# Long-convolution weights on TensorE: half-zero weights replaced by full ones

## The chip, the core and the metric

The kernel runs on one core of one Trainium2 chip. The metric is device time in microseconds (us); lower is better. The engines are named as in the profile: PE (TensorE matmul) and PEld (its weight loads), DVE (VectorE), ACT (ScalarE), POOL (GpSimd) and SP (SyncE, which here only issues DMAs).

## What is computed

Two independent halves are computed and concatenated along the last axis, each of shape 1 x 2048 x 512, in bf16.

```python
# A: attention, 32 heads of 16
qkv = (x @ wqkv).reshape(B, S, 3, 32, 16)
p = softmax(einsum("bhqd,bhkd->bhqk", q, k) * 16 ** -0.5)
a = einsum("bhqk,bhkd->bhqd", p, v).reshape(B, S, 512) @ wo
# B: gated long convolution, 512 channels
k_shift = sum_t k_pad[:, t:t+S] * shift_k[:, 3 - t]        # 4 taps
kv = k_shift * v
y = causal_conv(kv, ssm_k) + kv * ssm_D                     # 2048 taps per channel
b = q * y
```

The reference does the causal convolution by FFT; the kernel does it directly on PE.

## The kernel before

**Attention.** There are 2,048 blocks of scores, each 128 keys by 512 queries of one head (line 679). A loop over steps T (line 1429) emits the program; it is a planner written in Python that keeps a model time for each engine and decides at build time which instruction comes next on which engine. Each step takes up to three blocks into one of two sets of three PSUM banks (`emit_qk`, L796 is the scores matmul); ACT turns the whole set into exponentials with one instruction (L821), 128 x 1536 for three blocks or 128 x 1024 for two, into places of the ring PT. Two steps later the products with V follow (L970), four heads side by side in column groups, all accumulated in bank PVB; each finished group of 64 blocks is transposed on DVE (L1041).

**Blocks on DVE.** DVE computes the exponential of some blocks itself. `dve_block` chooses one, `exp_on_dve` emits it: L884 reads the scores out of PSUM, then on pairs of blocks follow four kinds of steps, `mant` (L892, into FR), `power` (L896), `line` (L899), `square` (L902) and `cube` (L905). The result has three parts, so each such block needs three product matmuls (ring PTD, R_PTD = 3 pairs of three tiles). A DVE block comes either beside a full set of three ACT blocks, in bank BGB, or in place of the third ACT block, in its bank (`own`, lines 726 to 730; this is tried when the DVE work in store is under LOW). BGB is refused while a convolution burst or a unit holds it (`busy`), and while a burst wants to begin (`conv_wants`).

**The convolution.** The zero-padded, reversed filters lie in HBM as kz_scratch. `feed_wr` (L1157) loads the rows of the ring WR: partition i of the lower 64 holds the filter of one channel shifted by i, the upper 64 partitions the filter of the channel 64 rows further on. `conv_lags` (L1187) multiplies, for a group `qd` of 8 channels, KV (weights) with WR (moving): KV has the time blocks of one channel on the lower and of the other channel on the upper half, in alternate columns, with zeros in the other half of each column. 64 groups x 32 lags x 4 column groups make 8,192 matmuls. Two groups form a burst in BGB; its end is a copy with reversed order to YB on DVE (L1207). After every fourth group four transposes (L1219, the "turn") and one product with Q (L1226) follow.

**Inputs of the convolution.** Units `("kv", c, i)` compute the 4-tap shift as matmuls with diagonal weights (L512) and multiply with V on DVE (L561, two instructions per unit); `spread_kv` then spreads the result over the partitions with four DMAs per unit group.

**Order.** Other background work comes as units with due steps (`jobs`, from PLAN steps). `emit_bg` gives the convolution up to LAGS = 10 lags per step if the room before the next ACT end allows it. `release` issues filter rows by the modelled DMA rate (WR_KB, line 122) and so that they do not collide with PE's fetches of its own code. A burst may begin only WAIT = 3.0 us (line 106) after the modelled landing of its rows (line 1337). Where nothing else fits, `warm_up` (L1382) puts filler matmuls on PE. The last N_TAIL = 9 steps have two blocks each.

Of the kernel before, what the change touches and what calls it, by code (L numbers as in the profile page):

```python
# [27 lines left out]
NLAG = S // 64  # L28
# [4 lines left out]
R_W = 12  # L33
R_PT = 16
# [8 lines left out]
LEAD = 2  # L43
YIELD = -4
FIRST = 6
BURST = 2
OVER_C = 0.0
HURRY = 2
LOW = 4.5
# [20 lines left out]
R_PTD = 3  # L70
# [12 lines left out]
PLAN = 588  # L83
# [4 lines left out]
GAP = 5  # L88
# [7 lines left out]
DMA_KB = 394  # L96
X_KB = 200
# [157 lines left out]
def bass_concat_heads__mha_block__ssm_conv_h3__prompt_kernel(  # L255
# [24 lines left out]
    def sb(name, shape, dt=BF16):  # L280
# [9 lines left out]
    WR = sb("WR", [128, R_W, S])  # L290
    WRF = WR[:, :, :].rearrange("p r w -> p (r w)")
    KV = sb("KV", [128, C // 8, 2, 2 * NB, 4])
    QNF = sb("QN", [128, NB * 256 + 2 * LEFT])
    QN = QNF[:, 0:NB * 256].rearrange("p (t d) -> p t d", t=NB)
# [13 lines left out]
    PTD = sb("PTD", [128, R_PTD, 3, 2, QB])  # L308
    FR = sb("FR", [128, 2 * QB])
# [7 lines left out]
           for x in (WR[:, R_W - 2, :], WR[:, R_W - 1, :], OUTA[:, :, :].rearrange("p r d -> p (r d)"), VS2[:, :])]  # L317
# [9 lines left out]
    KVF = KV[:, :, :, :, :].rearrange("p o r u g -> p (o r u g)")  # L327
    STG = [KVF[:, 32 * S // 16 * ((c + 1) % 4):32 * S // 16 * ((c + 1) % 4 + 1)].rearrange(
        "p (h o u k g) -> p h o u k g", h=2, o=16, u=NB, k=2) for c in range(4)]
    XN = FR[:, :].rearrange("p (j f) -> p j f", j=2)  # L330
# [66 lines left out]
    d_wr = [DmaSem(sem(f"d_wr{i}")) for i in range(3)]  # L397
# [25 lines left out]
    for c in range(4):  # L423
        src = bass.AP(tensor=v2.tensor, offset=v2[128 * (NB - 1), 128 * c].offset, ap=[[D, 128], [-128 * D, NB], [1, 128]])
        h_vn.append(dma(sp, d_kv[3 + c], VST[c], src, kb=512))
# [18 lines left out]
    h_kv0 = [None, None]  # L444
    h_kv0[0] = pool.op(lambda e: e.memset(KV[:, :, :, :, :].rearrange("p o r u g -> p (o r u g)").bitcast(U32), 0), us=(8.8, 8.9))
# [25 lines left out]
    def ready(u):  # L471
        if u[0] == "q":
            return (u[1] < R_Q or 2 * (u[1] - R_Q) + 1 in qk_done) and (u[1] < 2 or 2 * u[1] - 1 in h_q and at(h_q[2 * u[1] - 1]) <= pe.t + 0.5)
        if u[0] == "k":
            return u[1] < 2 or LAST[u[1] - 2] in qk_done
        if u[0] == "v":
            return u[1] < 2 or LAST[u[1] - 2] in pv_done
        if u[0] == "op":
            return (PAIRS.index((3, u[1])) if u[1] < NQB - 1 else (15, u[2] + 1)) in h_otn and h_wop[0] is not None
        return KT_OF[u[1]][0] in h_kt and (u[1] < 3 or h_kv0[1] is not None and at(h_kv0[1]) <= pe.t)  # L480

    def pe_unit(u, bank, parts=(0, 1, 2, 3)):
# [19 lines left out]
        elif kind == "kv":  # L502
# [5 lines left out]
            def mm(e, b):  # L508
                ins = None
                for m in range(4):  # L510
                    c0 = LEFT + 128 * (4 * i + 3 - b) - m
                    ins = e.matmul(PS[:, bank, 128 * b:128 * b + 128], lhsT=KTR[kt_i][:, kt_c, c0:c0 + 128], rhs=DG[:, c, m, :],  # L512
                                   start=(m == 0), stop=(m == 3))
# [20 lines left out]
    def evac_unit(u, bank, h):  # L534
# [18 lines left out]
        elif kind == "kv":  # L553
            _, c, i = u
            u0 = NB - 4 - 4 * i
            val = VST[c][:, u0:u0 + 4, :].rearrange("p b (h o g) -> p b h o g", h=2, g=4)
            src = PS[:, bank, :].rearrange("p (b h o g) -> p b h o g", b=4, h=2, g=4)
            for ch in range(2):
                dst = STG[c][:, ch, :, u0:u0 + 4, ch, :].rearrange("p o u g -> p u o g")
                hh = (dve.op if ch else urgent)(  # L560
                    lambda e, dst=dst, ch=ch: e.tensor_tensor(dst, src[:, :, ch], val[:, :, ch], ALU.mult),  # L561
                    [h, h_vn[c], h_kv0[c // 3]], us=(0.335, 0.46))
# [3 lines left out]
            if sum(kv_n[0:2]) == 8 and c < 2:  # L566
                load_qn(0, [h])
                open_wr(2, hh, True)
# [13 lines left out]
    def spread_kv(c, hh):  # L582
        for half in range(2):
            for ch in range(2):
# [23 lines left out]
    def kz_store(us):  # L608
# [4 lines left out]
        open_wr(R_W - 2, h_kzw[0])  # L613
# [111 lines left out]
    def emit_qk(T):  # L725
# [12 lines left out]
        bl = next_blocks(n + (extra in next_blocks(n)))  # L738
        if extra in bl:
            bl.remove(extra)  # L740
# [30 lines left out]
    def next_blocks(n):  # L771
        bl = []
        for b in [b for b in queue[:LOOK] if blk_group(b) == blk_group(queue[0])] + queue[:n]:
            if len(bl) < n and b not in bl and (blk(b)[2] not in [blk(x)[2] for x in bl] or len(bl) + 1 > 4):
                bl.append(b)
        for b in queue[:n]:
# [58 lines left out]
    def conv_due():  # L835
        return N_OPEN + state["qd"] * (PLAN - N_OPEN) / (C // 8)

    def conv_wants(T):
        qd = state["qd"]
        return (state["started"] and T >= conv_due() - YIELD and qd < C // 8 and wr_next[0] >= qd + BURST and h_kvc[qd // 16] is not None  # L840
                and at(h_wr[qd + BURST - 1], h_kvc[qd // 16]) + WAIT < pe.t + 1.0 and not (state["turn"] and qd % 4 == 4 - BURST))

# [3 lines left out]
    def dve_block(T, n_act, aside=True):  # L846
        if T < T_DVE or aside and busy() or len(queue) < LAST_BLKS + 3 * TAIL_GAP + 4:
            return None
        if aside and conv_wants(T):
# [9 lines left out]
        bl = next_blocks(n_act + 1)  # L859
        x = sub(bl[-1])  # L860
        left = len([b for b in queue if sub(b) == x])
        if left - 3 >= 2.6 * GAP:
            return bl[-1]
# [6 lines left out]
        rows = [blk(b)[2] for b in bl[:-1]]  # L870
        ahead = [b for b in ahead[:4] if b not in bl]
        return next((b for b in ahead if blk(b)[2] not in rows), ahead[0] if ahead else None)
# [5 lines left out]
    def exp_on_dve(b, bank, h):  # L878
# [4 lines left out]
        lin, low, top = [PTD[:, j % R_PTD, i, :, :].rearrange("p a n -> p (a n)") for i in range(3)]  # L883
# [7 lines left out]
        def mant(us):  # L891
            st["d"] = st["m"] = dve.op(lambda e: e.tensor_scalar(FR[:, w].bitcast(U16), lin[:, w].bitcast(U16), 0x7F, 0x3F80, ALU.bitwise_and, ALU.bitwise_or),  # L892
                                       [st["h"][-1], h_last.get(j - 1)], us=us)

        def power(us):
            dve.op(lambda e: e.tensor_scalar(low[:, w].bitcast(U16), lin[:, w].bitcast(U16), 0xFF80, None, ALU.bitwise_and), [st["h"][-1]], us=us)  # L896

        def line(us):
            st["d"] = dve.op(lambda e: e.tensor_scalar(top[:, w].bitcast(FP16), FR[:, w], T1, T0, ALU.mult, ALU.add), [st["m"]], us=us)  # L899

        def square(us):
            st["d"] = h_last[j] = dve.op(lambda e: e.tensor_tensor(top[:, w].bitcast(FP16), FR[:, w], top[:, w].bitcast(FP16), ALU.mult), [st["d"]], us=us)  # L902
# [6 lines left out]
        begin = lambda: (n == 2 or st["alone"]) and (j == 0 or j - 1 in h_last)  # L909
        if half == 0:  # L910
            flow.append([])
            st["f"] = flow[-1]
        st["f"][:] = [("p", dep, mant, FOUR[n], begin), ("p", lambda: [st["h"][-1]], power, FOUR[n], lambda: True), ("p", lambda: [st["m"]], line, FOUR[n], lambda: True),
                      ("p", dep, square, TWO[n], lambda: True), ("p", dep, cube, TWO[n], lambda: True)]
# [26 lines left out]
    def emit_pv(bl, T):  # L941
# [5 lines left out]
        for b in bl:  # L947
            n, _, s = blk(b)
            pv_n[(n, s)] = pv_n.get((n, s), 0) + 1
            terms = [PTD[:, on_dve[b][0] % R_PTD, i, on_dve[b][1], :] for i in range(3)] if b in on_dve else [PT[:, pt_of[b], :]]  # L950
# [567 lines left out]
```

## Time and profile before

| | |
|---|---|
| median of 3 runs | 815.03 us (811.89 to 816.54) |
| the profiled execution | 807.64 us |
| its span in the profile | 805.7 us |
| busy: PE / DVE / ACT / POOL | 745.7 / 715.1 / 784.9 / 90.4 us |
| granted PE clock, mean | 0.999 |

A line of the groups reads: line, engine, operation, output <- input, shapes, number; then busy time in us and mean length of one in ns; then the idle time of the engine just before these instructions and who ended it. Instructions overlap on an engine's pipeline, so number times mean can exceed busy time. A line of the waits reads: who waited <- for whom: us in total, times, longest. A line of the timeline reads: start, length, engine, line, operation, number merged.

### The profile page before, as it was taken

What the parts mean: (1) busy time and instruction counts of PE and PEld (TensorE: products, weight loads), DVE (VectorE), ACT (ScalarE), POOL (GpSimd) and SP (SyncE); (2) the same over time, 40 slices, a digit from 0 to 9 for tenths busy, and PEclk for the clock granted to TensorE, in tenths of its full rate; (3) what the DMA queues carried; (4) which work ended last, traced back from release to release, by engine and by line L of the source; (5) the groups of instructions that cost most, each with busy time, mean ns of one, the idle gap of its engine ahead of it and who ended that gap; (6) DMA issues with size and microseconds to landing.
All of it is one profiled execution on the core that took longest, in us unless ns stands there. A gap on an engine that the chain in (4) does not pass through costs nothing.

```text
span 805.7 us, 31982 instructions
## 1 busy us (share of the span) xinstructions
PE 745.7 (93%) x14505; PEld 337.1 (42%) x14505; DVE 715.1 (89%) x1427; ACT 784.9 (97%) x680; POOL 90.4 (11%) x160
## 2 busy tenths in 40 slices
PE   8889998999998989999999989989989899999987
PEld 3333444435444433444433434434443434434444
DVE  5989999999798989898898989889999899889986
ACT  7999999999999999999999999999999999999997
POOL 6200402020100101020010030101003020000000
PEclk9999999999999999999999999999999999999999
DMA  9995277846877671446845657985684663876310
GB/s 244 204 306 175 63 184 227 287 108 215 265 261 240 215 243 59 156 115 235 267 142 206 213 168 254 308 281 193 227 299 138 212 224 129 283 260 216 110 55 28
DMA packets 88101, 161.44 MB, mean 200 GB/s; under 512 B 49216, under 2 KB 53184, under 8 KB 87584
## 3 DMA queue, kind: packets, MB, share of 16 engines
q1 hardware_dynamic: 80976, 150.43, 58.2%
q0 software_dynamic: 5792, 8.66, 3.7%
q8 instruction: 114, 1.87, 0.9%
q10 hardware_dynamic: 1200, 0.33, 0.2%
q14 instruction: 19, 0.16, 0.1%
HBM read 142.87 MB, written 6.42 MB: 185 GB/s over the span
## 4 chain that ended last, share of the span: by engine, by line
ACT 79%; PE 14%; DVE 5%; issue 1%; DMA 1%
ACT PT L821 79%; PE PS L970 5%; PE PS L796 4%; PE PS L1187 1%; DVE PTD L884 1%; DMA QN<-in_B_k_dram 1%; PE PS L512 1%; PE PS L1115 1%; PE PS L630 0%; PE PS L491 0%; DVE PTD L902 0%; DVE DT L1041 0%; DVE PTD L905 0%; DVE FR L892 0%; DVE PTD L896 0%
## 5 line engine op out<-in xcount | busy, mean ns | idle before, releaser
L821 ACT ACTIVATE PT<-PS 128x1024 bf16<-128x1024 f32 (+1 forms) x674 | 781.9, 1362 | 11.5 <-PE PS L796 10.8
L796 PE MATMUL PS<-QT,KTo 32*128 32x512 bf16 (+2 forms) x2248 | 265.6, 364 | 39.8 <-ACT PT L821 17.5
L884 DVE TENSOR_SCALAR PTD<-PS 128x512 uint16<-128x512 f32 x326 | 219.2, 682 | 49.2 <-PE PS L796 47.8
L1187 PE MATMUL PS<-WR,KV 128*26 128x128 bf16 (+9 forms) x8192 | 191.2, 219 | 0.7 <-issue 0.6
L970 PE MATMUL PS<-PT,VA 128*32 128x512 bf16 (+2 forms) x1889 | 184.6, 369 | 5.0 <-DVE DT L1041 2.1
L1187 PEld LDWEIGHTS PS<-WR,KV 128*32 128x32 bf16 (+8 forms) x8192 | 140.6, 94 | 52.9 <-issue 29.8
L796 PEld LDWEIGHTS PS<-QT,KTo 32*128 32x128 bf16 x2248 | 69.6, 91 | 205.0 <-ACT PT L821 150.4
L970 PE MATMUL PS<-PTD,VA 128*32 128x512 bf16 (+1 forms) x1077 | 121.0, 360 | 3.9 <-issue 3.9
L902 DVE TENSOR_TENSOR PTD<-FR,PTD 128x1024 f16<-128x1024 bf16 (+1 forms) x164 | 112.3, 685 | 4.0
L905 DVE TENSOR_TENSOR PTD<-PTD 128x1024 bf16<-128x1024 f16 (+1 forms) x164 | 111.5, 680 | 1.9
L352 POOL DMA_DIRECT2D QT<-QS x120 | 60.4, 511 | 443.7 <-DVE QS L539 443.7
L970 PEld LDWEIGHTS PS<-PT,VA 128*32 128x32 bf16 x1889 | 47.4, 93 | 100.8 <-issue 85.5
L892 DVE TENSOR_SCALAR FR<-PTD 128x1024 uint16<-128x1024 uint16 (+1 forms) x164 | 69.0, 421 | 3.5
L896 DVE TENSOR_SCALAR PTD<-PTD 128x1024 uint16<-128x1024 uint16 (+1 forms) x164 | 68.9, 420 | 0.0
L1382 PE MATMUL PS<-IDN,ZW 128*32 128x512 bf16 (+3 forms) x297 | 67.4, 310 | 1.3 <-issue 1.0
L899 DVE TENSOR_SCALAR PTD<-FR 128x1024 f16<-128x1024 bf16 (+1 forms) x164 | 68.1, 415 | 0.0
L970 PEld LDWEIGHTS PS<-PTD,VA 128*32 128x32 bf16 x1077 | 44.8, 96 | 33.2 <-issue 4.4
L1382 PEld LDWEIGHTS PS<-IDN,ZW 128*32 128x32 bf16 x297 | 23.4, 96 | 23.3 <-issue 12.2
L1041 DVE STREAM_TRANSPOSE DT<-PS 128x512 f32<-128x512 f32 x31 | 22.1, 713 | 5.6 <-PE PS L970 5.3
L352 POOL DMA_DIRECT2D out_dram<-OUTA x15 | 8.6, 575 | 97.2 <-DVE OUTA L1123 93.1
L1115 PE MATMUL PS<-WKV,OTN 128*128 128x512 bf16 (+1 forms) x68 | 19.0, 371 | 0.3 <-DVE OTN L1090 0.3
L523 PE MATMUL PS<-WKV,xT 128*128 128x128 bf16 x256 | 18.3, 220 | 0.4 <-DVE KTo L548 0.3
(75 smaller groups left out, 259.3 us busy)
## 6 DMA issues: line engine op xcount, KB each, us to landing
WR<-kz_scratch SPq DMA_DIRECT2D x256, 512.0 KB, 5.8
KV<-KV SPq DMA_DIRECT2D x16, 256.0 KB, 5.4
kz_scratch<-WR SPq DMA_DIRECT2D x1, 2176.0 KB, 8.8
QN<-in_B_q_dram POOLq DMA_DIRECT2D x2, 1024.0 KB, 7.6
out_dram<-QN POOLq DMA_DIRECT2D x2, 1024.0 KB, 8.3
QT<-QS POOLq DMA_DIRECT2D x120, 16.0 KB, 3.3
out_dram<-OUTA POOLq DMA_DIRECT2D x15, 128.0 KB, 2.0
QN<-in_B_ssm_k_dram SPq DMA_DIRECT2D x1, 1024.0 KB, 8.3
```

Of the source, the lines that this page charges most:

```text
L352: f(outp, inp).then_inc(dsem.sem, 16)
L796: ins = e.matmul(PS[:, bank, i * w:i * w + w], lhsT=KTo[32 * s:32 * s + 32, OF[n_] % 2, kt * 128:(kt + 1) * 128], rhs=QT[32 * s:32 * s + 3 ...
L821: h_exp[T] = act.op(lambda e: e.activation(PT[:, p0:p0 + n, :].rearrange("p b f -> p (b f)"), PS[:, banks[0]:banks[0] + n, :].rearrange("p ...
L884: st["h"].append(urgent(lambda e: e.tensor_scalar(lin[:, QB * half:QB * half + QB].bitcast(U16), PS[:, bank, :], FIX_ADD, FIX_HI, ALU.add, ...
L892: st["d"] = st["m"] = dve.op(lambda e: e.tensor_scalar(FR[:, w].bitcast(U16), lin[:, w].bitcast(U16), 0x7F, 0x3F80, ALU.bitwise_and, ALU.b ...
L896: dve.op(lambda e: e.tensor_scalar(low[:, w].bitcast(U16), lin[:, w].bitcast(U16), 0xFF80, None, ALU.bitwise_and), [st["h"][-1]], us=us)
L899: st["d"] = dve.op(lambda e: e.tensor_scalar(top[:, w].bitcast(FP16), FR[:, w], T1, T0, ALU.mult, ALU.add), [st["m"]], us=us)
L902: st["d"] = h_last[j] = dve.op(lambda e: e.tensor_tensor(top[:, w].bitcast(FP16), FR[:, w], top[:, w].bitcast(FP16), ALU.mult), [st["d"]], ...
L905: st["d"] = dve.op(lambda e: e.tensor_tensor(top[:, w], top[:, w].bitcast(FP16), lin[:, w], ALU.mult), [st["d"]], us=us)
L970: ins = e.matmul(dst, lhsT=w, rhs=rhs, start=first, stop=last, tile_position=(0, 32 * s))
L1187: ins = e.matmul(PS[32 * g:32 * g + 2 * ((30 - d) // 2 + 1), BGB, c0:c0 + w], lhsT=kv, rhs=WR[:, (4 * qd + g) % R_W, S - 64 * d - 128:S - ...
L1382: pe.op(lambda e, s=s, k=k, rhs=rhs, bank=bank, rows=rows, c0=c0, first=first: e.matmul(PS[32 * s:32 * s + rows, bank, c0:c0 + 128 * k], l ...
```

## The change

Each channel's 2,048 time steps are now 32 blocks of 64. The lower 64 partitions of WR hold lags of one channel, the upper 64 the lags 1024 further on of the same channel; KV holds on its upper half the same time blocks 1024 earlier, so no weight is zero by construction, apart from the blocks before the start of time. A group `qd` is 4 channels, there are 128 groups of 8 steps, and each matmul covers two lags of 64, whose results are added when YB is turned: the turn is now two matmuls with permuted identity columns per 128 columns instead of one transpose, into fp32. Four groups form a burst.

A filter row of WR is half as long (1,024 columns); a DMA writes 64 partitions of two rows. The ring has 24 rows of half the length, so the same bytes. The kv units write KV directly with one DVE instruction, and one DMA per unit group makes the upper half. Q and the convolution's output move in two DMAs each, 128 channels wide.

Beside that, the blocks on DVE get other rings (R_PTD = 5 for the first tile, R_RST = 3 for the two others; FR is gone and `mant` writes into the second tile, `power` comes after `square`), PT has 14 places instead of 16, blocks are chosen so that the blocks of a step lie in different head rows (`next_blocks`, `pick_row`), `conv_wants` refuses a DVE block only if the last attempt found room for lags or the convolution is over 30 steps behind, and several planner constants have other values.

```diff
-NLAG = S // 64
+NLAG = S // 256
+NQD = C // 4
-R_W = 12
-R_PT = 16
+R_W = 24
+R_PT = 14
+PRESS = 30
-FIRST = 6
-BURST = 2
+FIRST = 4
+BURST = 4
-LOW = 4.5
+LOW = 3.5
-R_PTD = 3
+R_PTD = 5
+R_RST = 3
-PLAN = 588
+PLAN = 600
-GAP = 5
+GAP = 7
...
-    PTD = sb("PTD", [128, R_PTD, 3, 2, QB])
-    FR = sb("FR", [128, 2 * QB])
+    PTD = sb("PTD", [128, R_PTD, 2, QB])
+    RST = sb("RST", [128, R_RST, 2, 2, QB])
...
 kv unit
-                    c0 = LEFT + 128 * (4 * i + 3 - b) - m
-                    ins = e.matmul(PS[:, bank, 128 * b:128 * b + 128], lhsT=KTR[kt_i][:, kt_c, c0:c0 + 128], rhs=DG[:, c, m, :],
-                                   start=(m == 0), stop=(m == 3))
+                    for x in range(2):
+                        c0 = LEFT + 64 * (4 * i + 3 - b) + S // 2 * x - m
+                        ins = e.matmul(PS[64 * x:64 * x + 64, bank, 128 * b:128 * b + 128], lhsT=KTR[kt_i][:, kt_c, c0:c0 + 64],
+                                       rhs=DG[:, c, m, :], start=(m == 0), stop=(m == 3), tile_position=(0, 64 * x))
...
 spread_kv
-        for half in range(2):
-            for ch in range(2):
-                src = STG[c][64 * half:64 * half + 64, ch].rearrange("p o u k g -> p o (u k g)")
-                dst = KV[ch:128:2, 16 * c:16 * c + 16, 1 - half, :, :].rearrange("p o u g -> p o (u g)")
-                h_kvc[c] = dma(sp, d_kvc[c], dst, src, [hh, h_kvc[c - 1] if c else None] if half + ch == 0 else [], kb=256, rate=210)
+        src = KV[0:64, 32 * c:32 * c + 32, 0:NB, :].rearrange("p q w g -> p q (w g)")
+        dst = KV[64:128, 32 * c:32 * c + 32, NB:2 * NB, :].rearrange("p q w g -> p q (w g)")
+        h_kvc[c] = dma(sp, d_kvc[c], dst, src, [hh, h_kv0, h_kvc[c - 1] if c else None], kb=256, rate=KV_KB)
...
 dve_block
-        if aside and conv_wants(T):
+        if aside and conv_wants(T) and (state["go"] or conv_due() < T - PRESS):
...
 feed_wr
-            qd, g = n // 4, n % 4
-            row = 128 * (qd // 16) + 4 * (qd % 16) + g
-            src = bass.AP(tensor=kz_ap.tensor, offset=kz_ap[row, 0].offset, ap=[[1, 64], [64 * LKZ, 2], [1, S]])
-            h_wr[qd] = dma(sp, d_wr[qd % 3], WR[:, n % R_W, :], src, [h_kzw[0], dep, h], kb=512, rate=WR_KB, late=2.95)
+            qd, r, x = n // 4, n % 4 // 2, n % 2
+            src = bass.AP(tensor=kz_ap.tensor, offset=kz_ap[channel(qd) + 2 * r, S // 2 * x].offset, ap=[[1, 64], [LKZ, 2], [1, S // 2]])
+            n0 = (4 * qd + 2 * r) % R_W
+            h_wr[qd] = dma(sp, d_wr[qd % (R_W // 4)], WR[64 * x:64 * x + 64, n0:n0 + 2, :], src, [h_kzw[0], dep, h], kb=256, rate=WR_KB, late=2.95)
...
 conv_lags
-                d = DIST[n]
-                w = 64 if d < 0 else 128
                 for g in range(4):
-                    kv = KV[:, qd, (1 + d) % 2, (1 + d) // 2 * 2:2 * NB, g]
-                    ins = e.matmul(PS[32 * g:32 * g + 2 * ((30 - d) // 2 + 1), BGB, c0:c0 + w],
-                                   lhsT=kv, rhs=WR[:, (4 * qd + g) % R_W, S - 64 * d - 128:S - 64 * d - 128 + w],
+                    dst = PS[32 * g:32 * g + 32 - 2 * n, BGB, :]
+                    c0 = 256 * (1 - pair) + 64 * (1 - half)
+                    dst = bass.AP(tensor=dst.tensor, offset=PS[32 * g:32 * g + 1, BGB, c0:c0 + 1].offset, ap=[dst.ap[0], [128, 2], [1, 64]])
+                    w0 = S // 2 - 128 * n - 128
+                    ins = e.matmul(dst, lhsT=KV[:, channel(qd) // 4, 2 * n:2 * NB, g], rhs=WR[:, (4 * qd + g) % R_W, w0:w0 + 128],
                                    start=(n == 0), stop=(n == NLAG - 1), tile_position=(0, 32 * g))
...
 conv_turn
-                ins = e.transpose(pbf[:, 128 * k:128 * k + 128], YB[:, b % 2, 128 * k:128 * k + 128], IDN[:, :])
+                for part in range(2):
+                    y = YB[:, k // 2, 256 * (k % 2) + 128 * part:256 * (k % 2) + 128 * part + 128]
+                    ins = e.matmul(PS[:, bank, 128 * k + 4 * part:128 * k + 128], lhsT=y, rhs=(own, next_)[part], start=part == 0, stop=part == 1)
```

More of the change, by code (lines that the diff above doesn't have):

```diff
@@ L479, in ready @@
             return (PAIRS.index((3, u[1])) if u[1] < NQB - 1 else (15, u[2] + 1)) in h_otn and h_wop[0] is not None
[L480 removed]
+        return KT_OF[u[1]][0] in h_kt
     def pe_unit(u, bank, parts=(0, 1, 2, 3)):
@@ L869, in dve_block @@
             return None
-        rows = [blk(b)[2] for b in bl[:-1]]
-        ahead = [b for b in ahead[:4] if b not in bl]
-        return next((b for b in ahead if blk(b)[2] not in rows), ahead[0] if ahead else None)
+        return pick_row(ahead, 4)
     h_last = {}
@@ L908, in exp_on_dve @@
         dep = lambda: [st["d"]]
-        begin = lambda: (n == 2 or st["alone"]) and (j == 0 or j - 1 in h_last)
+        begin = lambda: (n == 2 or st["alone"]) and (j < R_RST or all((j - R_RST, i) in h_ptd for i in range(len(pairs[j - R_RST]["h"]))))
         if half == 0:
@@ L949, in emit_pv @@
             pv_n[(n, s)] = pv_n.get((n, s), 0) + 1
-            terms = [PTD[:, on_dve[b][0] % R_PTD, i, on_dve[b][1], :] for i in range(3)] if b in on_dve else [PT[:, pt_of[b], :]]
+            terms = [PT[:, pt_of[b], :]] if b not in on_dve else [PTD[:, on_dve[b][0] % R_PTD, on_dve[b][1], :]] + [
+                RST[:, on_dve[b][0] % R_RST, i, on_dve[b][1], :] for i in range(2)]
             hl = 2 * s + n % 2
@@ L991, in conv_done @@
     def conv_done():
-        return state["qd"] == C // 8 and not state["turn"] and not part[0]
+        return state["qd"] == NQD and not state["turn"] and not part[0]
     def pv_step(T):
@@ L1213, in conv_turn @@
     def conv_turn(b, bank):
-        pbf = PS[:, bank, :].bitcast(BF16)
+        own, next_ = [bass.AP(tensor=IDN[:, :].tensor, offset=IDN[0:1, 31:32].offset, ap=[IDN[:, :].ap[0], [-1, n], [32, 4]]) for n in (32, 31)]
         def fn(e):
```

163 lines of the change are left out of this document (86 added, 77 removed).

## The prediction

> **What bounds the kernel now.** I read the engine totals first, then the chain that ended last, then the groups with their forms kept apart, then the waits.
>
> ```profile
> PE 745.7 (93%) x14505; PEld 337.1 (42%) x14505; DVE 715.1 (89%) x1427; ACT 784.9 (97%) x680; POOL 90.4 (11%) x160
> ...
> ACT 79%; PE 14%; DVE 5%; issue 1%; DMA 1%
> ...
> L821 ACT ACTIVATE PT<-PS 128x1024 bf16<-128x1024 f32 (+1 forms) x674 | 781.9, 1362 | 11.5 <-PE PS L796 10.8
> ```
>
> ScalarE (ACT) is occupied for 784.9 of 805.7 us, and the chain runs through it for 79% of the span. Its exponential (L821) loses 11.5 us to idling in all, nearly all of it waiting for scores (L796). So the time can fall in two ways only: ACT idles less, or ACT gets less to do. The forms show what its work is made of:
>
> ```profile
> L821 ACT ACTIVATE PT<-PS 128x1536 bf16<-128x1536 f32 x374 | 524.9, 1558 | 2.8 <-PE PS L796 2.5
> L821 ACT ACTIVATE PT<-PS 128x1024 bf16<-128x1024 f32 x300 | 301.1, 1117 | 8.7 <-PE PS L796 8.3
> ...
> L884 DVE TENSOR_SCALAR PTD<-PS 128x512 uint16<-128x512 f32 x326 | 219.2, 682 | 49.2 <-PE PS L796 47.8
> ...
> L902 DVE TENSOR_TENSOR PTD<-FR,PTD 128x1024 f16<-128x1024 bf16 x162 | 111.4, 688 | 4.0
> L905 DVE TENSOR_TENSOR PTD<-PTD 128x1024 bf16<-128x1024 f16 x162 | 110.6, 683 | 1.9
> ...
> L892 DVE TENSOR_SCALAR FR<-PTD 128x1024 uint16<-128x1024 uint16 x162 | 68.4, 422 | 3.4
> L896 DVE TENSOR_SCALAR PTD<-PTD 128x1024 uint16<-128x1024 uint16 x162 | 68.3, 422 | 0.0
> L899 DVE TENSOR_SCALAR PTD<-FR 128x1024 f16<-128x1024 bf16 x162 | 67.6, 417 | 0.0
> ```
>
> There are 2,048 score blocks. ACT takes 374 x 3 + 300 x 2 = 1,722, VectorE (DVE) the other 326. A third block makes an ACT instruction 1558 - 1117 = 441 ns longer. 1,722 x 0.441 = 759.4 us; the remaining 22.5 us of the 781.9 are spread over 674 instructions, 33 ns each. So **a block moved to DVE is worth 0.441 us, an instruction saved 0.033 us**. A block costs DVE 682 + (688 + 683 + 422 + 422 + 417)/2 = 1,998 ns, say 2.0 us. DVE is 89% busy, and over half of its 90.6 idle us, 47.8, is spent in front of L884 with no block of scores at hand. What DVE lacks is blocks in time; that is where the change has to act.
>
> Now what the convolution takes from TensorE (PE):
>
> ```profile
> L1187 PE MATMUL PS<-WR,KV 128*26 128x128 bf16 (+9 forms) x8192 | 191.2, 219 | 0.7 <-issue 0.6
> ```
> ```profile
> 210.92 0.29 PE L1187 MATMUL PS<-WR,KV 128*26 128x128 bf16 x8
> ...
> 213.75 0.74 PE L1187 MATMUL PS<-WR,KV 128*16 128x128 bf16 x40
> 214.74 0.71 PE L1187 MATMUL PS<-WR,KV 128*6 128x128 bf16 x40
> 216.27 0.73 PE L1187 MATMUL PS<-WR,KV 128*28 128x128 bf16 x40
> ```
>
> Four column groups run side by side: 32 more matmuls lengthen a run by 0.45 us, 14 ns each, whether the weights have 6, 16 or 28 columns. 8,192 of them are 115 us of PE's pace, the largest part that isn't attention.
>
> **The change, part by part.**
>
> *Convolution on PE.* 64 x 32 lags x 4 become 128 x 8 x 4 = 4,096 matmuls. The weights that remain are the wide ones (32 to 18 columns), which the rows above show to cost no more. Gain: 57 us.
>
> ```profile
> L523 PE MATMUL PS<-WKV,xT 128*128 128x128 bf16 x256 | 18.3, 220 | 0.4 <-DVE KTo L548 0.3
> ...
> L512 PE MATMUL PS<-OTN,QN 128*128 128x128 bf16 x128 | 9.4, 220 | 1.6 <-DMA QN<-in_B_k_dram 1.0 <-DVE KV L561 0.3 <-DVE PTD L884 0.3
> L512 PE MATMUL PS<-OTN 128*128 128x128 bf16 x128 | 9.2, 220 | 0.7 <-DVE KV L561 0.7
> ```
>
> *Turn and kv units on PE.* The turn (L1219) gets 128 matmuls for 64; at the 18.3/256 = 71 ns of L523 that is +4.6 us. The kv units (L512) get 512 half-wide ones for 256; in two column groups they should run in pairs as the convolution's fours do, so +0; one after the other they would cost another 18.6 us. I take 0. PE sheds about 57 - 5 = 52 us. None of that is saved time by itself: PE isn't the bound, and the warm-up filler (L1382) will occupy part of it.
>
> *DVE.* The copy from PSUM (L1207) stays at 32 instructions but doubles to 512 columns:
>
> ```profile
> L1207 DVE CAST YB<-PS 128x256 bf16<-128x256 f32 x32 | 13.3, 416 | 5.8 <-PE PS L1187 3.0 <-PE PS L970 2.3 <-PE PS L1382 0.4
> ...
> L575 DVE CAST VA<-PS 128x512 bf16<-128x512 f32 x16 | 10.9, 681 | 1.5 <-PE PS L523 1.5
> ...
> L561 DVE TENSOR_TENSOR KV<-PS,WR 128x256 bf16<-128x256 f32 x16 | 6.0, 413 | 2.0 <-PE PS L512 2.0
> ```
>
> 32 x (681 - 416) = +8.5 us. The kv products (L561) go from 32 of 413 ns to 16 of about 681: -2.3 us. The other DVE steps of a pair keep their number and shape. Net +6.2 us of DVE work.
>
> *Rings of DVE blocks.* The first result of a pair gets five places instead of three, the other two tiles get their own ring of three, and the shared FR tile with its order between pairs is gone. Two more pairs are four L884, 2.7 us of work that can be taken while the ring behind is full.
>
> ```profile
> DVE PTD L884 <- PE PS L796: 47.8, 67, 3.3
> ```
>
> The longest of these 67 waits is 3.3 us, so most fit into that lead; but the four fifths of the arithmetic that follow still wait for a ring of three. I take 30 of the 47.8 us as gained (ends: 0 and 47.8).
>
> *The bank BGB.* DVE blocks beside a full ACT instruction need this bank, and a convolution burst holds it:
>
> ```profile
> 208.87 0.24 PE L1187 MATMUL PS<-WR,KV 128*32 128x128 bf16 x1
> ...
> 226.68 0.25 PE L1187 MATMUL PS<-WR,KV 128*32 128x128 bf16 x1
> ```
> ```profile
> 222.80 0.41 DVE L1207 CAST YB<-PS 128x256 bf16<-128x256 f32 x1
> ...
> 238.16 0.42 DVE L1207 CAST YB<-PS 128x256 bf16<-128x256 f32 x1
> ```
>
> 13.9 and 11.5 us are held in bursts that come 15 to 18 us apart. That is why 300 ACT instructions have two blocks: the third bank went to DVE. There are still 32 bursts, of 32 lags in place of 64, so the hold should halve. I estimate that a third of the pairs become triples.
>
> *PT with 14 places for 16.* Cost nothing: the waits name no ACT wait for a product (L970) that frees a place. If that cover goes, a wait is about one product group, 0.40 us; 1,711 blocks go round some 143 times at four triples a round, and one late round in ten would be 6 us. Kept in the range.
>
> *DMA.* The filter rows keep their bytes; 512 issues of 256 KB replace 256 of 512 KB, and a row piece is 2 KB instead of 4. SP pays 256 more issues of about 0.61 us, 155 us on an engine that does nothing else in that time.
>
> ```profile
> DMA packets 88101, 161.44 MB, mean 200 GB/s; under 512 B 49216, under 2 KB 53184, under 8 KB 87584
> ...
> q0 software_dynamic: 5792, 8.66, 3.7%
> ```
> ```profile
> L352 SPq DMA_DIRECT2D WR<-kz_scratch x256: 512/606/1702, 50.5 to 751.0; - x128
> ```
> ```profile
> DMA packets 4179, 14.56 MB, mean 291 GB/s; under 512 B 558, under 2 KB 686, under 8 KB 4167
> ...
> q1 hardware_dynamic: 3911, 14.26, 84.7%
> ```
>
> The last fence is the busiest 50 us stretch (500 to 550). There a packet of 3.65 KB took 0.847 x 16 x 50 / 3911 = 173 ns; those of q0, 1.50 KB on average over the span, took 0.037 x 16 x 805.7 / 5792 = 82 ns. On the line between them 2 KB take 105 ns and 4 KB 192, so the same bytes take 10% longer. The mean DMA load rises by some 5 points; the waits show no convolution waiting for rows, so I cost it at nothing and take the loss of that cover as a rival. Q and the convolution's output go in 256-byte rows; they are needed once per half of the channels. The KV spread shrinks from 16 DMAs to 4.
>
> [...]
>
> **The sum.** DVE gains 30 - 6.2 = 23.8 us, 12 blocks: ACT loses 12 x 0.441 = 5.3 us. The 1,710 blocks left to ACT, with 200 pairs, are 437 triples: 637 instructions, 37 fewer, 1.2 us. ACT's 10.8 us of waits for scores halve, 5.4 us. What such a wait looks like:
>
> ```profile
> 142.99 0.58 PE L1187 MATMUL PS<-WR,KV 128*24 128x128 bf16 x27 [0.64 <-issue]
> 143.50 0.10 PEld L796 LDWEIGHTS PS<-QT,KTo 32*128 32x128 bf16 x3
> ...
> 143.94 2.37 ACT L821 ACTIVATE PT<-PS 128x1024 bf16<-128x1024 f32 x2 [0.38 <-PE PS L796]
> ```
>
> The scores stand in PE's queue behind convolution lags that began late. With half the lags and fewer instructions to fetch this is rarer, but PE is also given more DVE blocks (three product terms each), so I take half. Together 5.3 + 1.2 + 5.4 = **11.9 us**: the span falls to 793.8, the profiled execution from 807.64 to about 795.7. The median shown, 815.03 (811.89 to 816.54), lies 7.4 us above the profiled one; I carry the difference over: 815.03 - 11.9 = **803 us**.
>
> **The rivals.**
>
> *DVE fills up (gain larger).* If all 47.8 us go, DVE gains 41.6 us, 20 blocks, 8.8 us; all pairs but the tail's 9 become triples, 570 instructions, 3.4 us; and most of ACT's waits go, 10 us. 815 - 22 = 793. For it: no block needs anything but a bank, a ring place and PE. Against it: a ring of three still gates the arithmetic, and bursts, units and turns still compete for BGB.
>
> *The ring of three binds as before (no change).* DVE gains nothing and pays 6.2 us, three blocks, +1.4 us for ACT; the instructions and a quarter of the waits bring 3.9. 812.5 us. It would also come out so if PE's pace were not set by the number of convolution matmuls, and so the conversion saved little. For it: DVE's idle time is spread over 67 waits, which speaks for a rule of order more than a lack of PE time.
>
> *Filter rows come late (slower).* The planner (line 122) reckons 330 KB per us; the stretch above moved 291 GB/s at 87% load, 335 at full load, and 10% longer packets make it 304. Each 256 KB then lags by 0.066 us, and the plan leaves 3.0 us (line 106) between landing and first use. After 45 rows back to back, 11.5 MB, that is used up; the stretch above did move 14.26 MB on this queue in 50 us. From there each burst of 16 rows is 1.1 us later; PE runs in order, so scores stand behind it and ACT idles with it. For half of 32 bursts that is 17 us: 815 - 12 + 17 = 820. Against it: only few stretches are so full; the mean is 200 GB/s.
>
> **How the numbers follow.** Forecast, 0.53. Larger gain, 0.21. No change, 0.13. Late rows, 0.13. A run of this kernel can be told from no change beyond about 0.5%, 4 us: faster 0.74, same 0.13, slower 0.13. The range is 788 to 816: it takes in the larger gain with some room for DVE blocks beyond it, the loss by PT and the case of no change, and leaves out late rows.
>
> **What would show it.** L1187 has 4,096 matmuls and about half of 191 us. L821 has fewer instructions than 674 and more triples than 374. L884 has about 338 blocks and some 20 us of idle time before it in place of 49. L1207 takes about 0.68 us. ACT's waits for L796 are near 5 us. Wrong would be: L884 at 326 or fewer, its idle time still near 48; a wait of L1187 or L796 for the DMA of WR; an ACT wait for L970; or PEclk below 9 where PE has less to do.

## The result, and the profile after

| | before | after |
|---|---|---|
| median | 814.88 us (811.89 to 816.54, 4 runs) | 882.30 us (872.84 to 884.95, 4 runs) |
| profiled execution, its span | 807.64, 805.7 us | 884.95, 883.1 us |
| mean granted TensorE clock in it | 0.999 | 0.934 |

The changed kernel is 8.1% slower: the ratio is 1.0811, 95% interval 1.0719 to 1.0903. The forecast was 803 us with a range of 788 to 816, so neither the sign nor the range held.

The page of the kernel after, from the engine totals down to the DMA issues (in a group's row: busy time and mean ns of one, then the idle time ahead of it and what ended most of it):

```profile
PE 775.3 (88%) x10969; PEld 308.6 (35%) x10969; DVE 753.8 (85%) x1501; ACT 780.5 (88%) x636; POOL 90.7 (10%) x163
...
PEclk9999997998699896999799998999999999989999
...
q1 hardware_dynamic: 109520, 147.30, 73.0%
...
ACT 44%; PE 33%; DVE 17%; issue 5%; DMA 1%; SPq 0%
...
L821 ACT ACTIVATE PT<-PS 128x1536 bf16<-128x1536 f32 (+2 forms) x630 | 777.6, 1363 | 93.9 <-PE PS L796 92.6
...
L888 DVE TENSOR_SCALAR PTD<-PS 128x512 uint16<-128x512 f32 x351 | 239.3, 683 | 39.3 <-PE PS L796 37.8
...
L1199 PE MATMUL PS<-WR,KV 128*18 128x128 bf16 (+7 forms) x4096 | 96.1, 228 | 16.2 <-issue 13.9
...
L1215 DVE CAST YB<-PS 128x512 bf16<-128x512 f32 x32 | 21.9, 685 | 17.3 <-PE PS L1199 16.1
L1228 PE MATMUL PS<-IDN,YB 128*128 128x128 bf16 (+1 forms) x128 | 30.1, 389 | 1.9 <-DVE YB L1215 0.9
L1235 DVE TENSOR_TENSOR QN<-PS,QN 128x512 bf16<-128x512 f32 x16 | 11.1, 691 | 23.3 <-PE PS L1228 23.3
...
WR<-kz_scratch SPq DMA_DIRECT2D x512, 256.0 KB, 8.2
```

The work went as planned: half the convolution matmuls, 351 blocks on DVE in place of 326, 630 exponentials in place of 674, and ACT 4.4 us less busy. But ACT is now idle for 883.1 - 780.5 = 102.6 us, against 20.8 before. 92.6 of these are waits for scores (10.8 before). This rise of 81.8 us, less the 4.4, is the whole 77.4 us of the longer span. TensorE delivers late, and the question is why. Two rows stand out. The filter queue q1 moves fewer bytes than before (147.30 MB against 150.43) but keeps the DMA engines for 73.0% of a longer span (58.2% before). And the turn, L1228, is busy for 30.1 us. The queue's row on the page of the kernel before:

```profile
q1 hardware_dynamic: 80976, 150.43, 58.2%
```

The view of waits of the kernel after (engine, line, what it waited for: us in total, times, longest):

```profile
PEld PS L975 <- issue: 113.3, 388, 4.4
...
ACT PT L821 <- PE PS L796: 92.6, 102, 4.4
...
DVE RST L896 <- PE PS L975: 19.1, 18, 4.1
...
PE PS L1199 <- issue: 13.9, 6, 3.9
...
PE PS L796 <- issue: 9.9, 6, 3.6
```

PE waits 13.9 us in six pieces before convolution matmuls, 9.9 us in six before scores and 8.8 us in four before products, for nothing that the profile names ("issue"). The longest of these stalls take 3 to 4 us, and the longest waits of ACT and DVE are about as long. In the kernel before, PEld's waits of this kind had much the same number, but none was long:

```profile
PEld PS L970 <- issue: 89.9, 372, 1.5
```

The totals by stretch of the kernel after (window, length, busy us and count of PE, PEld, DVE, ACT and POOL, granted clock, DMA share, GB/s):

```profile
150.00:200.00 50.00, 41.87 (x651) 16.49 (x648) 39.62 (x79) 40.70 (x33) 4.41 (x8) 0.89 1.05 233
200.00:250.00 50.00, 42.04 (x478) 14.97 (x475) 35.69 (x70) 37.58 (x31) 3.73 (x7) 0.80 0.88 195
250.00:300.00 50.00, 46.34 (x697) 18.64 (x693) 48.10 (x97) 49.59 (x43) 4.96 (x10) 1.00 0.44 101
600.00:650.00 50.00, 45.12 (x647) 17.30 (x644) 42.99 (x85) 45.40 (x37) 4.05 (x8) 0.97 1.07 256
```

Where the DMA engines are full or nearly so, ACT is busy for 38 to 45 of 50 us and the clock is below 1. Where they aren't (third line), ACT is busy for 49.59 us at full clock. And full means only 233 to 256 GB/s here (first and last line); the stretch that the prediction quoted moved 291 at 87%.

One stall in the timeline of the kernel after (start, us, engine, line, count, in brackets the idle time before it):

```profile
181.13 0.39 PE L796 MATMUL PS<-QT,KTo 32*128 32x512 bf16 x2 [2.38 <-issue]
...
181.57 1.45 ACT L821 ACTIVATE PT<-PS 128x1536 bf16<-128x1536 f32 x1 [2.33 <-PE PS L796]
181.83 1.29 PE L1199 MATMUL PS<-WR,KV 128*20 128x128 bf16 x40
...
186.40 1.87 PE L1228 MATMUL PS<-IDN,YB 128*128 128x128 bf16 x8
...
188.31 0.69 DVE L1235 TENSOR_TENSOR QN<-PS,QN 128x512 bf16<-128x512 f32 x1 [1.37 <-PE PS L1228]
```

PE stands still for 2.38 us and ACT for 2.33. The 40 convolution matmuls after it take 1.29 us, where in the kernel before they took 0.71 to 0.74: the clock has fallen, and the stall is paid a second time. The totals around it show the granted clock, the third number from the right:

```profile
178.00:181.40 3.40, 0.65 (x3) 0.18 (x3) 1.74 (x4) 1.23 (x2) 0.00 (x0) 1.00 1.07 273
181.60:184.90 3.30, 3.30 (x58) 1.56 (x50) 1.62 (x3) 2.44 (x2) 0.00 (x0) 0.50 1.02 209
```

The granted clock was 1.00 up to the end of the stall of 2.38 us and 0.50 behind it. Further down in the timeline, one turn of eight matmuls takes 1.87 us, and DVE waits for it.

### The profile page after: what moved, and what is told of

Read it like the earlier page. It is cut to its first block, busy times and chain, and to the rows that moved or that the text cites. A ratio compares the mean times of both kernels' runs of the same rounds, so it can differ in the third digit from the quotient of the medians.

```text
span 883.1 us, 25210 instructions
## 1 busy us (share of the span) xinstructions
PE 775.3 (88%) x10969; PEld 308.6 (35%) x10969; DVE 753.8 (85%) x1501; ACT 780.5 (88%) x636; POOL 90.7 (10%) x163
## 3 DMA queue, kind: packets, MB, share of 16 engines
q1 hardware_dynamic: 109520, 147.30, 73.0%
## 4 chain that ended last, share of the span: by engine, by line
ACT 44%; PE 33%; DVE 17%; issue 5%; DMA 1%; SPq 0%
ACT PT L821 44%; PE PS L975 12%; PE PS L796 9%; DVE PTD L888 5%; PE PS L1228 3%; PE PS L1199 3%; PE PS L1396 3%; DVE RST L909 2%; DVE RST L903 2%; DVE RST L896 2%; DVE RST L906 1%; DVE DT L1046 1%; DVE RST L900 1%; DMA WR<-kz_scratch 1%; PE PS L1120 1%
## 5 line engine op out<-in xcount | busy, mean ns | idle before, releaser
L821 ACT ACTIVATE PT<-PS 128x1536 bf16<-128x1536 f32 (+2 forms) x630 | 777.6, 1363 | 93.9 <-PE PS L796 92.6
L1396 PE MATMUL PS<-IDN,ZW 128*32 128x512 bf16 (+3 forms) x481 | 121.2, 348 | 0.0
L903 DVE TENSOR_TENSOR RST<-RST 128x1024 f16<-128x1024 bf16 (+1 forms) x177 | 119.6, 677 | 1.8
L909 DVE TENSOR_TENSOR RST<-RST,PTD 128x1024 bf16<-128x1024 f16 (+1 forms) x177 | 119.4, 676 | 0.0
L1199 PE MATMUL PS<-WR,KV 128*18 128x128 bf16 (+7 forms) x4096 | 96.1, 228 | 16.2 <-issue 13.9
L975 PE MATMUL PS<-RST,VA 128*32 128x512 bf16 (+1 forms) x774 | 102.9, 380 | 2.7 <-issue 2.7
L896 DVE TENSOR_SCALAR RST<-PTD 128x1024 uint16<-128x1024 uint16 (+1 forms) x177 | 74.6, 424 | 19.7 <-PE PS L975 19.1
L1199 PEld LDWEIGHTS PS<-WR,KV 128*18 128x18 bf16 (+7 forms) x4096 | 73.2, 104 | 41.5 <-issue 29.6
L975 PE MATMUL PS<-PTD,VA 128*32 128x512 bf16 (+1 forms) x387 | 75.5, 384 | 2.9 <-issue 2.9
L900 DVE TENSOR_SCALAR RST<-RST 128x1024 f16<-128x1024 bf16 (+1 forms) x177 | 73.2, 416 | 1.9
L906 DVE TENSOR_SCALAR RST<-PTD 128x1024 uint16<-128x1024 uint16 (+1 forms) x177 | 73.7, 417 | 0.9
L1228 PE MATMUL PS<-IDN,YB 128*128 128x128 bf16 (+1 forms) x128 | 30.1, 389 | 1.9 <-DVE YB L1215 0.9
L1235 DVE TENSOR_TENSOR QN<-PS,QN 128x512 bf16<-128x512 f32 x16 | 11.1, 691 | 23.3 <-PE PS L1228 23.3
```

The lines of the kernel that those rows point to most:

```text
L821: h_exp[T] = act.op(lambda e: e.activation(PT[:, p0:p0 + n, :].rearrange("p b f -> p (b f)"), PS[:, banks[0]:banks[0] + n, :].rearrange("p ...
L896: st["d"] = dve.op(lambda e: e.tensor_scalar(low[:, w].bitcast(U16), lin[:, w].bitcast(U16), 0x7F, 0x3F80, ALU.bitwise_and, ALU.bitwise_or ...
L903: st["d"] = dve.op(lambda e: e.tensor_tensor(top[:, w].bitcast(FP16), low[:, w], top[:, w].bitcast(FP16), ALU.mult), [st["d"]], us=us)
L909: st["d"] = dve.op(lambda e: e.tensor_tensor(top[:, w], top[:, w].bitcast(FP16), lin[:, w], ALU.mult), [st["d"]], us=us)
L975: ins = e.matmul(dst, lhsT=w, rhs=rhs, start=first, stop=last, tile_position=(0, 32 * s))
L1199: ins = e.matmul(dst, lhsT=KV[:, channel(qd) // 4, 2 * n:2 * NB, g], rhs=WR[:, (4 * qd + g) % R_W, w0:w0 + 128], start=(n == 0), stop=(n = ...
```

## The experiments

Three theories for the loss: **A**, the 2 KB pieces make the filter DMAs slow; **B**, it is their destination, 64 adjacent partitions; **C**, the turn is the main cause, because its moving operand, the permuted identity, is read in steps of 32 elements. Medians of the kernel before beside these runs were 814.8 to 816.2 us, so times of different experiments can be set side by side.

### e1: all 128 partitions per DMA, 2 KB pieces as in the change

```diff
-            src = bass.AP(..., offset=kz_ap[channel(qd) + 2 * r, S // 2 * x].offset, ap=[[1, 64], [LKZ, 2], [1, S // 2]])
-            n0 = (4 * qd + 2 * r) % R_W
-            h_wr[qd] = dma(..., WR[64 * x:64 * x + 64, n0:n0 + 2, :], src, ...)
+            src = bass.AP(..., offset=kz_ap[channel(qd) + 2 * r + x, 0].offset, ap=[[1, 64], [S // 2, 2], [1, S // 2]])
+            n0 = (4 * qd + 2 * r + x) % R_W
+            h_wr[qd] = dma(..., WR[:, n0, :], src, ...)
```

> The changed kernel, but each filter DMA writes all 128 partitions of one row (2 KB per partition) instead of 64 partitions of two rows; bytes, number of DMAs and piece size stay. The rows land in another order of partitions, so the convolution's values are not the reference's. Theory A (2 KB pieces are slow): filled stretches stay near 235 to 255 GB/s, time near 880 us. Theory B (64 partitions at a time are slow): filled stretches move over 320 GB/s, the load of the DMA queue falls from 73% to near 55%, and the time falls to about 830 us or less. Theory C (the slow turn, not the DMA, makes ACT idle): the time stays near 880 us whatever the DMA rate does.

Measured: 820.9 us (818.15 to 822.06, 8 runs), ratio 1.0065 (1.0039 to 1.009). Of the 67 us, 61 are gone. Its page:

```profile
q1 hardware_dynamic: 109520, 147.30, 57.6%
```

The same 109,520 packets of the same size take 57.6% of 820.2 us in place of 73.0% of 883.1: 472 us of all engines against 645. The stretch from 150 to 170 us in the DMA view, of after and then of e1 (packets, MB, share of 16 engines; the last line has the median us from issue to landing):

```profile
DMA packets 2523, 4.64 MB, mean 232 GB/s; under 512 B 277, under 2 KB 277, under 8 KB 2520
...
q1 hardware_dynamic: 2520, 4.59, 105.8%
...
WR<-kz_scratch SPq DMA_DIRECT2D x18, 256.0 KB, 10.8
```
```profile
DMA packets 4948, 6.52 MB, mean 326 GB/s; under 512 B 1888, under 2 KB 1888, under 8 KB 4943
...
q1 hardware_dynamic: 4943, 6.45, 99.1%
...
WR<-kz_scratch SPq DMA_DIRECT2D x21, 256.0 KB, 4.7
```

Both are full; one moves 232 GB/s, the other 326, with more small packets in it. And PE's stalls go with it. The waits of e1:

```profile
PEld PS L975 <- issue: 84.9, 356, 0.7
...
ACT PT L821 <- PE PS L796: 33.1, 62, 1.4
```

The longest "issue" wait of this kind falls from 4.4 to 0.7 us. A falls, B holds, and C can't be the main cause: the turn is unchanged here.

### e2: 64 partitions as in the change, but pieces of 4 KB

```diff
-            src = bass.AP(..., offset=kz_ap[channel(qd) + 2 * r, S // 2 * x].offset, ap=[[1, 64], [LKZ, 2], [1, S // 2]])
+            src = bass.AP(..., offset=kz_ap[channel(qd) + 2 * r + x, 0].offset, ap=[[1, 64], [1, S]])
-            h_wr[qd] = dma(..., WR[64 * x:64 * x + 64, n0:n0 + 2, :], src, ...)
+            h_wr[qd] = dma(..., WR[64 * x:64 * x + 64, n0:n0 + 2, :].rearrange("p r w -> p (r w)"), src, ...)
```

> The changed kernel, but each filter DMA reads 4 KB of one channel into the two adjacent rows of 64 partitions: the same bytes, DMAs and partitions, pieces of 4 KB instead of 2. The rows hold other taps, so the convolution's values are not the reference's. Theory A (2 KB pieces are slow): over 320 GB/s in filled stretches and about 830 us or less. Theory B (64 partitions at a time are slow): 235 to 255 GB/s and about 880 us. Theory C (the turn): about 880 us.

Measured: 886.1 us (885.34 to 886.81, 2 runs), ratio 1.0853 (1.0782 to 1.0923). Its page and the line of its waits:

```profile
q1 hardware_dynamic: 76752, 147.30, 70.5%
```
```profile
ACT PT L821 <- PE PS L796: 92.6, 97, 5.0
```

Three packets in ten are gone, and time, load and waits stay as they were. B again: the destination counts, not the piece.

### e3: the turn with an identity permuted once ahead of the loop

GpSimd writes the permuted identity once, so the turn reads it in steps of one element.

```diff
-        own, next_ = [bass.AP(..., offset=IDN[0:1, 31:32].offset, ap=[IDN[:, :].ap[0], [-1, n], [32, 4]]) for n in (32, 31)]
+        own, next_ = IDN[:, 0:128], IDN[:, 0:124]
```

> The changed kernel with the permuted identity of the turn laid out once, in plain order, at the start, so that the turn's matmuls read their moving operand in sequence; the output is the reference's. Expected in any case: the eight matmuls of a turn take about 0.6 us instead of 1.8 us, 19 us less on PE in sum over 16 turns. Theory A or B (DMA load is the main cause): the time falls by 5 to 20 us, to 862 to 877 us. Theory C (the turn is the main cause): ACT's waits of 92.6 us for scores fall below 30 us and the time to about 815 us.

Measured: 858.4 us (853.96 to 862.91, 2 runs), ratio 1.0514 (1.0369 to 1.066): about 24 us of the loss are gone, somewhat more than expected, by two runs that lie 9 us apart. A turn in its timeline, and below it one of the kernel before:

```profile
407.12 0.61 PE L1232 MATMUL PS<-IDN,YB 128*128 128x128 bf16 x8 [0.18 <-DVE YB L1219]
```
```profile
139.32 0.40 PE L1219 MATMUL PS<-IDN,YB 128*128 128x128 bf16 x4
```

Eight matmuls take 0.61 us in place of 1.87; per turn 1.26 us, over 16 turns 20 us. The filter DMAs are as in the change, and ACT still waits 72.5 us for scores. So C is a second cause, not the main one. The traces show what the step of 32 costs here (the pattern takes four elements 32 apart, then the next four, one back): (1.87 - 0.39) / 7 = 211 ns for each further matmul, against (0.61 - 0.22) / 7 = 56 ns with adjacent elements; 0.39 and 0.22 are the mean of one matmul alone in the groups of after (L1228, 389 ns) and e3 (223 ns).

### e4 and e5: the kernel before, with one property of the new DMAs each

e4 loads each row of the kernel before in two DMAs to all 128 partitions, in pieces of 2 KB; e5 in two DMAs to 64 adjacent partitions each, in pieces of 4 KB. (In the kernel before, the two channels of a row lie on alternate partitions, as the source pattern has it, and not on the two halves as its description ahead says. So each half in e5 holds half of the shifts of both channels.)

```diff
 e4
-            src = bass.AP(..., offset=kz_ap[row, 0].offset, ap=[[1, 64], [64 * LKZ, 2], [1, S]])
-            h_wr[qd] = dma(..., WR[:, n % R_W, :], src, ..., kb=512, ...)
+            for x in range(2):
+                src = bass.AP(..., offset=kz_ap[row, S // 2 * x].offset, ap=[[1, 64], [64 * LKZ, 2], [1, S // 2]])
+                h_wr[qd] = dma(..., WR[:, n % R_W, S // 2 * x:S // 2 * x + S // 2], src, ..., kb=256, ...)
 e5
+            for x in range(2):
+                src = bass.AP(..., offset=kz_ap[row, 32 * x].offset, ap=[[1, 32], [64 * LKZ, 2], [1, S]])
+                h_wr[qd] = dma(..., WR[64 * x:64 * x + 64, n % R_W, :], src, ..., kb=256, ...)
```

> The kernel before with every filter row loaded as two DMAs of half its columns, 2 KB per partition on all 128 partitions, instead of one of 4 KB; the output is the reference's. Theory A (2 KB pieces are slow): filled stretches move 235 to 255 GB/s, and the kernel before slows down to 850 us or more. Theory B (64 partitions) or C (the turn): filled stretches stay above 320 GB/s and the time stays within 10 us of 815 us.

> The kernel before with every filter row loaded as two DMAs of 64 adjacent partitions (4 KB per partition) instead of one of 128; the output is the reference's, the turn is the old one. Theory B (64 adjacent partitions at a time are slow): filled stretches move about 235 to 255 GB/s, code fetches and rows come late, and the time rises to 830 us or more. Rival (the slow rate needs the changed kernel's source pattern of two channels): filled stretches stay over 320 GB/s and the time within 6 us of 815 us.

Measured: e4 818.2 us (812.99 to 824.37, 8 runs), ratio 1.0042 (1.0005 to 1.008); e5 895.8 us (895.74 to 895.78, 2 runs), ratio 1.098 (1.0886 to 1.1073). The pages of e4 and of e5, with e5's waits:

```profile
q1 hardware_dynamic: 117840, 150.45, 59.9%
```
```profile
q1 hardware_dynamic: 85072, 150.45, 73.1%
```
```profile
DVE PTD L884 <- PE PS L796: 110.2, 80, 7.0
...
ACT PT L821 <- PE PS L796: 91.8, 82, 4.7
...
PE PS L970 <- issue: 25.7, 12, 4.1
```

Twice as many issues and smaller pieces cost 0.4%; the half range of partitions alone makes the old kernel, without any other part of the change, as slow as the new one and slower. The loss is well above the least that was expected of e5. The picture is the one of after: the DMA load at 73%, "issue" stalls of 4 us, ACT waiting 92 us.

### e7: 64 partitions, but every second one

Is it the number of partitions or their range? The one edit puts the rows on the even or the odd partitions.

```diff
-            h_wr[qd] = dma(..., WR[64 * x:64 * x + 64, n0:n0 + 2, :], src, ...)
+            h_wr[qd] = dma(..., WR[x:128:2, n0:n0 + 2, :], src, ...)
```

> The changed kernel, but each filter DMA writes every second partition of 128 (64 partitions, the even or the odd ones) instead of 64 adjacent ones; two channels, 2 KB pieces, bytes and number of DMAs stay. The rows land in another order of partitions, so the convolution's values are not the reference's. If the range of the partitions matters: over 320 GB/s in filled stretches and about 821 us, as with full-width DMAs. If their number matters: 235 to 255 GB/s and about 880 us.

Measured: 819.6 us (817.48 to 822.41, 8 runs), ratio 1.0043 (1.0011 to 1.0075). The DMA view of its stretch from 150 to 200 us:

```profile
DMA packets 9799, 14.12 MB, mean 282 GB/s; under 512 B 3023, under 2 KB 3151, under 8 KB 9790
...
q1 hardware_dynamic: 9534, 13.86, 86.1%
```

The queue's 13.86 MB in 50 us are 277 GB/s at 86.1% load, about 322 at full load and so near e1's 326. The range counts, not the number. In filled stretches 64 adjacent partitions moved 232 to 256 GB/s in after and 235 and 248 in e2, as streams of DMAs that take the two halves in turn; with every second partition the queue came near the rate of all 128. Why the range counts is not shown by any run.

### e6 and e8: the change with both causes taken away

e6 has the DMAs of e1 and the turn of e3. So that the convolution's other operand has the partition order of the full-width rows, the kv products go to a buffer STG first and are spread by three DMAs a group.

```diff
+        for x, par, w0 in ((0, 0, 0), (1, 1, 0), (0, 1, NB)):
+            src = STG[c][64 * x:64 * x + 64].rearrange("p q w g -> p q (w g)")
+            dst = KV[par:128:2, 32 * c:32 * c + 32, w0:w0 + NB, :].rearrange("p q w g -> p q (w g)")
+            h_kvc[c] = dma(sp, d_kvc[c], dst, src, ...)
```

> The changed kernel with both suspects taken away: filter DMAs of one row on all 128 partitions (KV gets the matching order of partitions by three small DMAs per channel group instead of one), and the turn with the plain permuted identity; the output is the reference's. Theory B plus the turn as the second cause: the first version with full-width DMAs had 820.9 us, the turn is worth 16 x 1.2 = 19 us at most where it delays scores; ACT's waits for scores fall to near 15 us and the time to 802 to 808 us, below the kernel before. Rival (what is left comes from the new rings, the smaller PT or the DVE load): ACT keeps over 25 us of waits and the time stays at 815 us or more.

Measured: 806.0 us (803.91 to 806.04, 4 runs), ratio 0.9871 (0.9804 to 0.9937). ACT is busy for 96% of the span again, and its waits for scores are down to 19.6 us. One of these waits stands out in the view of waits of e6, and beside it one of DVE's that would explain it: a group's products wait until the spread before has read the staging buffer that both use.

```profile
ACT PT L828 <- PE PS L803: 19.6, 30, 7.5
...
DVE KV L568 <- DMA KV<-KV: 5.9, 1, 5.9
```

e8 gives each group a staging buffer of its own, so that this wait goes:

```diff
-    STG = [KV[:, 64:96, 0:NB, :], KV[:, 96:128, 0:NB, :], KV[:, 96:128, 0:NB, :],
+    STG = [KV[:, 32:64, 0:NB, :], KV[:, 64:96, 0:NB, :], KV[:, 96:128, 0:NB, :],
-            hh = urgent(..., [h, h_vn[c], h_kvc[1] if c == 2 else None], us=V512)
+            hh = urgent(..., [h, h_vn[c]], us=V512)
```

> The version with full-width filter DMAs and the plain turn, with the kv results of the first three channel groups kept, before they are spread, in the KV regions of the next group, so that DVE does not wait there for an earlier spread (one wait of 5.9 us on DVE and 7.5 us on ACT in the version before). The output is the reference's. Theory (all that is left beside it is the ordinary work): ACT's waits for scores fall from 19.6 to about 12 us and the time from 806 to about 799 us. Rival (the 7.5 us would have been lost elsewhere, since DVE is the next to be full): the time stays within 2 us of 806 us.

Measured: 803.6 us (800.2 to 807.88, 6 runs), ratio 0.9886 (0.9846 to 0.9926). Its waits and its groups by form:

```profile
ACT PT L828 <- PE PS L803: 15.9, 25, 3.2
```
```profile
L828 ACT ACTIVATE PT<-PS 128x1536 bf16<-128x1536 f32 x447 | 625.0, 1573 | 6.5 <-PE PS L803 6.1
...
L895 DVE TENSOR_SCALAR PTD<-PS 128x512 uint16<-128x512 f32 x343 | 233.3, 683 | 9.6 <-PE PS L803 8.0
...
L828 ACT ACTIVATE PT<-PS 128x1024 bf16<-128x1024 f32 x182 | 194.8, 1126 | 10.4 <-PE PS L803 9.7
```

ACT's wait of 7.5 us is gone, so the shared staging buffer was its cause, as the order of the two waits in e6 has it (DVE from 113.1 to 119.0 us, ACT from 115.8 to 123.3). But the ranges of e6 and e8 overlap: whether removing it is worth the expected 7 us or nothing can't be told. Both are faster than the kernel before, by about 1.2%, a small gain that both intervals put above nothing.

## Why the prediction was wrong

**The step that failed is the one on DMA.** It priced the filter rows by the size of their pieces alone, 10% longer, and costed that at nothing. The size was right to call harmless: e4 measures 0.4% for the pieces and the extra issues together. What the step left out is where the rows land. All filter DMAs of before cover 128 partitions, so no row of its trace could show what 64 adjacent ones do; with no row the step should have had two bounds, and it had one number.

In place of some 304 GB/s at full load came 232 to 256. That is 61 us of the 67 (after to e1), and e2, e5 and e7 leave no other property of the DMA as the cause.

**The slower rival had the place but not the way.** It expected convolution matmuls that wait for their rows, 17 us. (It took 256 KB as 256,000 bytes; with 262,144 the lag of a DMA is 0.087 us in place of 0.066, and the 17 us are 22.) The rows are hardly waited for: in the PE waits of after there is one such wait.

```profile
PE PS L1199 <- DMA WR<-kz_scratch: 2.1, 1, 2.1
```

The loss is in PE's "issue" stalls and in the lower clock behind them. They come and go with the range of the rows (4.4 us at most in after, 0.7 in e1 for the same line).

What PE may wait for in these stalls can be read from the single DMA packets of the traces. The queue q8 carries blocks of 16 KB, 114 in the span of before and 87 in that of after:

```profile
q8 instruction: 87, 1.43, 0.7%
```

That is one block to 254 and to 252 of PE's instructions (matmuls and weight loads), which fits PE's own code. All 17 "issue" waits of PE over 0.3 us in after, 33 us together, end 1.3 to 2.2 us after the end of such a block, though a block comes only about every 10 us; the 26 longest of e5 end 1.3 to 1.8 us after one. In e1, with as many blocks, a single such wait is left, of 0.44 us. That PE stood still for code that came late is the author's reading of this order of events; no run moved the code itself. What would have held the blocks back is not shown: one block took 1.21 us on average in after and 1.10 in e1, a difference far shorter than the stalls. How much of the 61 us is the clock alone wasn't separated either; it stood at 0.50 for some 116 us in after, 24 in e1 and 55 in e3 (mean clocks 0.934, 0.985 and 0.968).

**The turn** was put at +4.6 us, at the pace of matmuls with adjacent operands. Its instructions read the identity in steps of 32 elements, and the 16 turns take 16 x 1.87 = 30 us, where before's took 16 x 0.40 = 6.4: +23.5 us. It stands in PE's order ahead of scores, and DVE waits 23.3 us for it (L1235). On top of the mended DMAs it is worth 15 us (e1 to e6, which also has another KV spread and 341 blocks on DVE in place of 351), by itself about 24 (after to e3).

**ACT's waits** were to halve to 5.4 us. They rose to 92.6; even in e6 and e8 they are 19.6 and 15.9, against 10.8 before, so this term had the wrong sign.

**What held.** 4,096 matmuls are busy for 96.1 us, half of 191.2. The copy takes 685 ns, 32 times (forecast 681). The kv units in half-wide pairs cost nothing more, in the groups by form of after 9.4 + 8.9 = 18.3 us against 18.6:

```profile
L515 PE MATMUL PS<-OTN,QN 128*64 128x128 bf16 x256 | 9.4, 221 | 0.8 <-DVE PTD L888 0.8
...
L515 PE MATMUL PS<-OTN 128*64 128x128 bf16 x256 | 8.9, 221 | 0.4 <-DVE PTD L888 0.4
```

And with both mis-sized terms taken away the sum comes out: e8 has 343 DVE blocks (forecast 338), 447 triples and 182 doubles, 629 instructions (forecast 437 triples, 637), and 803.6 us (forecast 803). The 12 us came about otherwise than forecast, though. DVE's idle time ahead of its first step fell further than assumed, to 9.6 us in place of some 20, so the new rings and the other changes to these blocks did more together (which of them wasn't separated); 17 blocks at 0.441 us are 7.5 us and 45 fewer instructions at 0.033 are 1.5, 9.0 together. ACT's waits take 5 us of it back. By these prices the span would fall by 4 us; it fell by 5.2 against the profiled execution of before, which was quicker than every other run of it shown here, and by about 11 in the medians. The rest was not traced. So it is in part luck that 803.6 meets 803: the forecast for the span was 793.8 us, and that of e8 is 800.5.

The ring of three is seen, as the rival of no change had it (DVE waits at the second step, L896, for products, 19.1 us in 18 pieces in after), but it doesn't decide the time: in e8 the same wait is 18.4 us, and that rival's 812.5 didn't come.

## What to carry to other kernels

Ahead of splitting a DMA, look at which partitions one DMA covers: 256 KB to 64 adjacent partitions held the engines about 1.4 times as long as the same bytes over 128, or over every second partition (645 us of all engines in after, 472 in e1, 0.558 x 820.7 = 458 in e7), while half the piece size cost 0.4% (e4). A transfer that is hardly waited for can still cost time (here 61 us, with one wait of 2.1 us for the rows): look at the clock, at "issue" waits and at ACT's idle time in the stretches where the DMA share is at 1, not at the waits for that DMA. And when a matmul gets a permuted operand by its access pattern, look at the step between elements of the moving operand before the number of matmuls (here 211 ns for each further one against 56).

## What the runs showed of the hardware that was not expected

- The rate of DMAs into SBUF by the range of partitions, at a load of one: 232 to 256 GB/s for 64 adjacent partitions (after, e2), 326 for 128 (e1), about 322 for 64 of every second (e7).
- TensorE's "issue" waits by where the filter DMAs land: the longest of a run is 4.4 to 5.0 us with 64 adjacent partitions (after, e2, e3, e5) and 0.8 to 1.9 in the other runs (0.8 in e1, on weight loads of scores, though its filter queue filled the engines to 99.1% from 150 to 170 us). In after each of PE's over 0.3 us ends 1.3 to 2.2 us after a 16 KB block on the instruction queue.
- In after the granted clock went to 0.50 behind a stall of 2.38 us, and its mean was 0.80 and 0.89 in stretches where PE was busy for 42 of 50 us.
- A 128-column matmul whose moving operand has a step of 32 bf16 elements takes some 211 ns against 56 with adjacent ones (after, e3).
